# Decays of an S4 convolution precomputed through DRAM, its parameter tables in one pass, and side stages traced at other marks

## Chip, cores and metric

One core of one Trainium2 chip runs the whole program. The metric is the device time of one execution in microseconds (us); the kernel before was timed three times, and a fourth execution was taken with the profiler on. Differences are compared between executions of the same kind, and a profiled execution has its own time beside the span that its trace covers.

## What is computed

A layer norm of `x` (2048 rows of 576 channels) feeds two branches whose results are added to `x`:

```python
xn = layernorm(x)                                  # (2048, 576)
# branch A: S4 convolution along the sequence, per channel d, 128 states n
dt = exp(log_dt);  logdA = dt * (A_re + 1j*A_im);  dB = dt * (B_re + 1j*B_im)
K[d, l] = sum_n (C_re + 1j*C_im)[d,n] * exp(logdA[d,n] * l) * dB[d,n]   # real part, l = 0..2047
y = causal convolution of xn with K (by FFT, length 4096) + xn * Dskip
# branch B: feed-forward
out = silu(xn @ w1) @ w2                           # 576 -> 4608 -> 576
return x + y + out
```

All inputs and outputs are fp32.

## The kernel before, in words

**Main work.** `ffn` (line 223) computes branch B. Each fp32 operand is split into a high and a low part, and three products replace one. The hidden dimension is cut into 9 chunks of 512 (`c`), the 2048 rows into two halves of two blocks of 512. For every block, the four `up` steps (line 273) make hidden tiles: 14 matmuls of 512 columns, then on ScalarE (ACT) a Silu (`gf`, line 289) and a rounding copy (`gh`, line 290), then on VectorE (DVE) the low part (`gl`, line 291). The four `down` steps (line 293) multiply by `w2`: 24 matmuls of 288 columns, and DVE adds the results to `acc` (line 310). The steps run u0, d0, d1, d2, d3, u1, u2, u3, where the ups belong to the next block, so between the Silu of u0 and that of u1 lie four down steps. There are 288 steps in all. The weights of the next chunk are split on ACT and DVE (lines 250, 252, 268, 270).

**Side work.** `side` (line 699) is a generator with everything else. `weave` (line 31) resumes it between two main steps when the main work has reached the fraction of the 288 steps that the generator yielded last. Its stages are:

1. `phase0` (line 194): load rows, normalise, transpose on TensorE (PE). Rows 0 to 7 before the main loop, rows 8 to 15 inside it.
2. `natural` (line 370): the parameter tables. In two halves of 96 partitions x 384 values it forms `dt*A`, and the modulus and phase of `C*dB`, and turns four tables by PE transposes (`ptk`, line 452) into the layout [128 states, 576 channels]: `lrT` (real part of the log decay), `fT`, `rhoT`, `phiT`. ACT uses Abs, Sqrt (line 426) and Arctan (line 434) for it; Sqrt and Arctan each bring an `ACT_TABLE_LOAD`, and so does the Silu that follows.
3. `kgen` (line 455): the response K in 36 chunks of 16 channels, in pairs. `powers` (line 478) makes, once a pair, the decays `exp(lr*256), exp(lr*64), exp(lr*8), exp(lr)` as (1+tanh)/(1-tanh): a product with the lags on DVE (line 484), Tanh on ACT (485), and 1-t, a reciprocal and a fused product on DVE (486, 487, 490), then their powers up to 7 (492 to 494). `head` makes phases, ACT their sines and cosines (517 to 521), DVE the products `S` and `C` (522 to 538), and PE the sums `kp` and `z` (558, 573). The results go to DRAM as `d1k`. `spread` (line 133) does the first FFT stage of `xn` beside it.
4. `spectral` (line 592): 32 iterations of loads, splits, PE products `pk`, `pu`, `pb` (line 671), results to DRAM `d2` (line 632).
5. `tail` (line 637): reads `d2` back as `ys` (line 678) with a lead of `AHEAD` = 6 row tiles, and `add_conv` (line 681) does the last FFT stage on PE (`py`, line 691) and adds it. Rows 0 to 7 are added here, rows 8 to 15 in the last `down` steps of `ffn`.

The marks in `side` say where stages 3 to 5 are traced: `marks = (0.14, 0.65, 0.875, 0.905, 0.945)` are the fractions of the main steps at which kgen begins, kgen ends and spectral begins, spectral ends, the tail begins and the tail ends.

**Order.** Engines run their instructions in a fixed order. A planner fixes it ahead of the run by simulating a timeline with its own cost estimates; an instruction traced earlier, or inside `tc.high_priority()`, goes first among those that are ready. `behind(ins)` (line 130) keeps an instruction behind `ins` on the same engine. All loads of the side stages go through SyncE's queue (SP), in which the weight loads stand too; GpSimd's queue (POOL) carries the `d1u` and `d2` writes.

Of the kernel before, what the change touches and what calls it, by code (L numbers as in the profile page):

```python
# [10 lines left out]
F32 = mybir.dt.float32  # L11
# [6 lines left out]
P = 128  # L18
# [23 lines left out]
def kernel(  # L42
# [40 lines left out]
    dr0 = dram.tile([8 * P, D], F32, name="dr0")  # L83

# [6 lines left out]
    nc.vector.memset(halfpi, math.pi / 2)  # L91
    mhalf = cst.tile([P, 2], F32, name="mhalf")
# [130 lines left out]
    def ffn():  # L223
# [38 lines left out]
        def split_w2(half, c, t):  # L262
            first = half == 0 and c == 0
            r2 = R2.pop((half, c, t))
            h2 = wp.tile([P, D], F32R, tag="w2h", name="w2h", bufs=FT + 1)
            l2 = wp.tile([P, D], F32R, tag="w2l", name="w2l", bufs=FT + 1)
            with behind(pins["xt_s"] if first else pins["gh"]):
                nc.scalar.copy(h2, r2)  # L268
            with behind(pins["w1l"] if first else None):
                nc.vector.tensor_sub(l2, r2, h2)  # L270
            W2[half, c, t] = h2, l2
# [98 lines left out]
    def natural(nat):  # L370
        lrT, fT, rhoT, phiT = (kf[n] for n in ("lr", "f", "rho", "phi"))
        for half in range(2):
            NT = 3
            NP = 96
            ts = slice(half * NT, (half + 1) * NT)

            def load(ap, name):
                t = nat.tile([NP, NT, NS], F32, tag=name, name=name)
                nc.sync.dma_start(t, ap.rearrange("(p t) n -> p t n", t=6)[:, ts, :])
                return t  # L380

            are, aim = load(a_re, "are"), load(a_im, "aim")
            br, bi = load(b_re, "br"), load(b_im, "bi")
            cr, ci = load(c_re, "cr"), load(c_im, "ci")
            dt = nat.tile([NP, NT], F32, tag="dt", name="dt")
            nc.sync.dma_start(dt, log_dt.rearrange("(p t) -> p t", t=6)[:, ts])

            e1 = nat.tile([NP, NT], F32, tag="e1", name="e1")
            e2 = nat.tile([NP, NT], F32, tag="e2", name="e2")
            ec = float(np.float32(math.e))  # L390
            nc.vector.memset(e1, ec)
            nc.vector.tensor_scalar(e2, dt, 1.0 - math.log(ec), 1.0, op0=ALU.mult, op1=ALU.add)
            nc.gpsimd.tensor_tensor(e1, e1, dt, op=ALU.pow)
            nc.vector.tensor_mul(dt, e1, e2)
            dtb = dt.unsqueeze(2).broadcast_to([NP, NT, NS])
            v = nc.vector

            def tl(name):
                return nat.tile([NP, NT, NS], F32, tag=name, name=name)

            dh = nat.tile([NP, NT], F32, tag="dh", name="dh")
            nc.vector.tensor_scalar(dh, dt, 0.5, None, op0=ALU.mult)
            dhb = dh.unsqueeze(2).broadcast_to([NP, NT, NS])
            v.tensor_mul(are, are, dtb)
            nc.scalar.mul(aim, aim, 1.0 / (2 * math.pi))
            v.tensor_mul(aim, aim, dtb)
            pr, pi, t0, t1 = tl("pr"), tl("pi"), tl("t0"), tl("t1")
            v.tensor_mul(pr, cr, br)
            v.tensor_mul(t0, ci, bi)
            v.tensor_sub(pr, pr, t0)  # L410
            v.tensor_mul(pi, cr, bi)
            v.tensor_mul(t0, ci, br)
            v.tensor_add(pi, pi, t0)

            nc.scalar.activation(cr, pr, AF.Abs)
            nc.scalar.activation(ci, pi, AF.Abs)
            v.tensor_tensor(br, cr, ci, op=ALU.max)
            v.tensor_tensor(bi, cr, ci, op=ALU.min)
            v.tensor_scalar(t0, br, 1e-37, None, op0=ALU.max)
            v.reciprocal(t0, t0)  # L420
            v.tensor_mul(t0, t0, bi)
            v.tensor_scalar(t0, t0, 1.0, None, op0=ALU.min)

            v.tensor_mul(t1, t0, t0)
            v.tensor_scalar(t1, t1, 1.0, None, op0=ALU.add)
            nc.scalar.activation(bi, t1, AF.Sqrt)
            rc = tl("rc")
            v.reciprocal(rc, bi)
            v.tensor_mul(rc, rc, t1)
            v.tensor_add(bi, bi, rc)  # L430
            v.tensor_mul(br, br, bi)
            v.tensor_mul(br, br, dhb)

            nc.scalar.activation(t0, t0, AF.Arctan)
            nc.scalar.mul(t0, t0, 1.0 / (2 * math.pi))
            v.tensor_tensor(rc, ci, cr, op=ALU.is_gt)
            v.tensor_scalar(t1, t0, -2.0, 0.25, op0=ALU.mult, op1=ALU.add)
            v.tensor_mul(t1, t1, rc)
            v.tensor_add(t0, t0, t1)
            v.tensor_scalar(rc, pr, 0.0, None, op0=ALU.is_lt)  # L440
            v.tensor_scalar(t1, t0, -2.0, 0.5, op0=ALU.mult, op1=ALU.add)
            v.tensor_mul(t1, t1, rc)
            v.tensor_add(t0, t0, t1)
            v.tensor_scalar(rc, pi, 0.0, None, op0=ALU.is_lt)
            v.tensor_scalar(rc, rc, 2.0, -1.0, op0=ALU.mult, op1=ALU.add)
            v.tensor_mul(t0, t0, rc)
            yield half
            for src, dst in ((are, lrT), (aim, fT), (br, rhoT), (t0, phiT)):
                dv = dst.rearrange("n (p t) -> n t p", t=6)
                pt = pss.tile([P, 512], F32, tag="pss", name="ptk")  # L450
                for i in range(3):
                    nc.tensor.transpose(pt[:, i * NP:(i + 1) * NP], src[:, i, :], ident[:NP, :NP])
                nc.scalar.copy(dv[:, ts, :], pt[:, :3 * NP].rearrange("n (i p) -> n i p", i=3))

    def kgen():
        lrT, fT, rhoT, phiT = (kf[n] for n in ("lr", "f", "rho", "phi"))
        with tc.tile_pool(name="kg", bufs=1) as kg:
# [19 lines left out]

            def powers(i):

                ms = kg.tile([P, 2, W, 4], F32, tag="ms", name="ms")  # L480
                md = kg.tile([P, 2, W, 4], F32, tag="md", name="md")
                al = kg.tile([P, 2, W, 4], F32, tag="al", name="al", bufs=2)
                for q in range(2):
                    nc.vector.tensor_mul(split(ms[:, q]), row(vt[:, 65:69], 4), col(lrT, i + q, 4))
                nc.scalar.activation(ms, ms, AF.Tanh, scale=0.5)
                nc.vector.tensor_scalar(md, ms, -1.0, 1.0, op0=ALU.mult, op1=ALU.add)
                nc.vector.reciprocal(md, md)
                pv = pw.rearrange("n r d k e -> n (r d k) e")
                R = 2 * W * 4
                nc.vector.scalar_tensor_tensor(pv[:, :, 1], ms.rearrange("n r d k -> n (r d k)"), 1.0,  # L490
                                               md.rearrange("n r d k -> n (r d k)"), op0=ALU.add, op1=ALU.mult)
# [206 lines left out]

    def side():
        nonlocal s4, kl, yp, pa  # L700
        marks = (0.14, 0.65, 0.875, 0.905, 0.945)
# [8 lines left out]
        with tc.tile_pool(name="kf", bufs=1) as kfp:  # L710
            for n in ("lr", "f", "rho", "phi"):
# [125 lines left out]
```

## Time and profile before

| | us |
|---|---|
| median of three runs | 1140.75 |
| the three runs | 1139.23, 1140.75, 1143.12 |
| profiled execution, its own time | 1136.48 |
| span of its trace | 1134.7 |
| VectorE busy in the span | 939.5 |
| ScalarE busy in the span | 708.0 |
| mean granted TensorE clock | 0.995 |

The profiled execution ran 4.3 us below the median of the runs. The busy time of PE counts a matmul from its start to its modelled end, and matmuls overlap, so a full PE row doesn't by itself mean that PE runs at its rate; gaps, waits and the granted clock have to be read beside it.

### The profile page before, as it was taken

How to read it: one execution, taken by the hardware profiler on the slowest of the kernel's cores; microseconds unless marked ns; L12 is line 12 of the kernel's file. 1: busy time of each engine (PE TensorE's matmuls, PEld its weight loads, DVE VectorE, ACT ScalarE, POOL GpSimd, SP SyncE). 2: the span in 40 equal slices, each digit the busy share in tenths (PEclk: the TensorE clock that was granted, in tenths of full speed). 3: DMA queues.
4: the chain of work that ended last, by engine and by line, in shares of the span. 5: the costliest groups of instructions: out<-in, count | busy, mean ns of one | idle time of the engine just before them, and what ended most of it. 6: DMA issues, size and time to landing. Idle time of an engine off the chain costs nothing.

```text
span 1134.7 us, 22990 instructions
## 1 busy us (share of the span) xinstructions
PE 1112.0 (98%) x9184; PEld 1003.2 (88%) x9184; DVE 939.5 (83%) x1649; ACT 708.0 (62%) x1236; POOL 71.7 (6%) x131
## 2 busy tenths in 40 slices
PE   6999999999999999999999999999999999999998
PEld 5988899998989898999898989899999999999957
DVE  7788899999999999999899995587778787777434
ACT  5454646656657666666666674578877777787400
POOL 2100000000000000000000000000000000000021
PEclk9999999999999999999999999999999999999989
DMA  8365312324215143456733242754545454442596
GB/s 261 115 187 187 114 32 79 80 89 99 92 53 127 64 93 96 93 179 173 217 80 109 67 103 57 214 154 141 162 136 152 132 180 144 147 139 74 163 269 196
DMA packets 156203, 148.89 MB, mean 131 GB/s; under 512 B 82512, under 2 KB 123616, under 8 KB 155584
## 3 DMA queue, kind: packets, MB, share of 16 engines
q1 hardware_dynamic: 145872, 110.30, 34.9%
q0 software_dynamic: 9840, 36.24, 9.6%
q8 instruction: 72, 1.18, 0.4%
q10 hardware_dynamic: 384, 0.89, 0.3%
q14 instruction: 35, 0.29, 0.1%
HBM read 102.56 MB, written 44.90 MB: 130 GB/s over the span
## 4 chain that ended last, share of the span: by engine, by line
PE 80%; DVE 7%; DMA 6%; issue 4%; ACT 2%; SPq 1%; ACTq 0%; DVEq 0%; POOLq 0%
PE po L306 34%; PE ph L281 28%; PE kp L558 3%; PE ph L283 2%; PE pk L671 2%; PE ph L282 2%; PE pu L671 2%; PE pb L671 2%; PE z L573 2%; DMA w1r<-in_B_w_dram 1%; PE py L691 1%; DMA ys<-d 1%; PE pu L149 1%; DMA w2r<-in_B_w_dram 1%; DMA acc<-in_A_u_dram 1%
## 5 line engine op out<-in xcount | busy, mean ns | idle before, releaser
L306 PE MATMUL po<-w2h,gh 128*128 128x288 f32 x1152 | 337.4, 297 | 2.5 <-ACT gh L290 2.0
L306 PE MATMUL po<-w2l,gh 128*128 128x288 f32 x1152 | 337.2, 296 | 0.0
L306 PE MATMUL po<-w2h,gl 128*128 128x288 f32 x1152 | 333.5, 296 | 0.6 <-DVE gl L291 0.6
L306 PEld LDWEIGHTS po<-w2h,gh 128*128 128x128 f32 x1152 | 215.2, 188 | 12.2 <-issue 2.8
L306 PEld LDWEIGHTS po<-w2l,gh 128*128 128x128 f32 x1152 | 215.8, 188 | 5.2 <-issue 0.9
L306 PEld LDWEIGHTS po<-w2h,gl 128*128 128x128 f32 x1152 | 214.4, 188 | 1.9 <-DVE gl L291 0.9
L281 PE MATMUL ph<-xh,w1h 128*128 128x512 f32 (+1 forms) x592 | 163.3, 392 | 0.3 <-ACT xh L119 0.3
L281 PE MATMUL ph<-xl,w1h 128*128 128x512 f32 (+1 forms) x592 | 161.6, 388 | 0.0
L281 PE MATMUL ph<-xh,w1l 128*128 128x512 f32 (+1 forms) x592 | 159.9, 386 | 0.0
L310 DVE TENSOR_TENSOR acc<-po,acc 128x288 f32<-128x288 f32 x288 | 126.5, 452 | 28.8 <-PE po L306 27.1
L289 ACT ACTIVATE gf<-ph 128x512 f32<-128x512 f32 (+1 forms) x148 | 86.4, 584 | 97.0 <-PE ph L283 83.9
L281 PEld LDWEIGHTS ph<-xl,w1h 128*128 128x128 f32 x592 | 109.6, 190 | 22.0 <-issue 0.9
L291 DVE TENSOR_TENSOR gl<-gf,gh 128x512 fp32r<-128x512 f32 (+1 forms) x148 | 99.1, 673 | 34.5 <-ACT gh L290 33.9
L281 PEld LDWEIGHTS ph<-xh,w1l 128*128 128x128 f32 x592 | 107.9, 188 | 20.9 <-issue 0.9
L281 PEld LDWEIGHTS ph<-xh,w1h 128*128 128x128 f32 x592 | 106.2, 192 | 16.8 <-issue 0.7
L290 ACT CAST gh<-gf 128x512 fp32r<-128x512 f32 (+1 forms) x148 | 90.0, 609 | 25.7 <-PE po L306 23.1
L517 ACT ACTIVATE c<-th,magic 128x1040 f32<-128x1040 f32 x36 | 42.1, 1169 | 48.2 <-DVE C L538 26.8
L252 DVE TENSOR_TENSOR w1l<-w1r,w1h 128x640 fp32r<-128x640 f32 x72 | 57.0, 818 | 5.7 <-ACT w1h L250 5.5
L519 ACT ACTIVATE c<-th 128x1040 f32<-128x1040 f32 x36 | 38.7, 1076 | 33.3 <-DVE th L518 33.1
L268 ACT CAST w2h<-w2r 128x576 fp32r<-128x576 f32 x72 | 46.9, 674 | 18.0 <-DMA w2r<-in_B_w_dram 14.6
L283 PE MATMUL ph<-x,w1l 128*128 128x512 f32 (+1 forms) x148 | 57.0, 385 | 0.0
L282 PE MATMUL ph<-x,w1h 128*128 128x512 f32 (+1 forms) x148 | 56.9, 385 | 0.0
(176 smaller groups left out, 1869.2 us busy)
## 6 DMA issues: line engine op xcount, KB each, us to landing
w2r<-in_B_w_dram SPq DMA_DIRECT2D x72, 288.0 KB, 3.0
w1r<-in_B_w_dram SPq DMA_DIRECT2D x35, 512.0 KB, 3.9
d1u<-u POOLq DMA_DIRECT2D x32, 288.0 KB, 2.7
d1k<-stage SPq DMA_DIRECT2D x18, 512.0 KB, 8.1
ur<-d1u SPq DMA_DIRECT2D x32, 288.0 KB, 3.6
kr<-d1k SPq DMA_DIRECT2D x32, 288.0 KB, 2.7
d<-yo POOLq DMA_DIRECT2D x32, 288.0 KB, 3.2
ys<-d SPq DMA_DIRECT2D x32, 288.0 KB, 11.0
```

What stands on the lines that cost most here:

```text
L252: pins["w1l"] = nc.vector.tensor_sub(l1, src, h1).ins
L268: nc.scalar.copy(h2, r2)
L281: nc.tensor.matmul(ph, w[:, kt, :], v[:, kt, a:e], start=n + kt == 0, stop=False)
L282: nc.tensor.matmul(ph, h1[:, 4, :], x4[:, a:e], start=False, stop=False)
L283: pins["pe"] = nc.tensor.matmul(ph, l1[:, 4, :], x4[:, a:e], start=False, stop=True).ins
L289: nc.scalar.activation(gf, ph, AF.Silu)
L290: pins["gh"] = nc.scalar.copy(gh, gf).ins
L291: pins["gl"] = nc.vector.tensor_sub(gl, gf, gh).ins
L306: pins["pe"] = nc.tensor.matmul(po[:, :HD], G[blk, t][g][:, js], W2[half, c, t][w][:, hs], start=n == 0, stop=n == 3 * FT - 1).ins
L310: nc.vector.tensor_add(acc[j][:, hs], po[:, :HD], acc[j][:, hs])
L517: nc.scalar.activation(c65, th, AF.Identity, bias=magic)
L671: nc.tensor.matmul(dst, st, mv[:, hs], start=n == 0, stop=n == 3 * len(terms) - 1)
```

## The change

- A DRAM tensor `dexp` and a constant `neg1` are added. The decays of all 576 channels and four lags are made once: Tanh on ACT from the turned table `lrT`, then 1/(t-1)^2 as the square of an absolute reciprocal root, one correction and the quotient on DVE in four slices; the result `ex` is written to `dexp`.
- `powers` no longer makes the decays. It loads a pair's 128 values per state (`eb`, a pair ahead, through SP) and ACT copies them into the power table `pw`.
- `natural` works on 96 x 768 values in one pass, cut by three yields. The second and the third ACT block that need other tables are placed by `gate_of` just behind the Silu and copy of a u0 step. The square root, its reciprocal and their sum (lines 426 to 430) become an absolute reciprocal root and five DVE instructions.
- The tables' parts and `phase0` of rows 8 to 15 are traced at new fractions, and the five marks become `(0.13, 0.58, 0.81, 0.915, 0.955)`.
- `norm` writes rows 8 to 15 over the loaded rows.

```diff
+    dexp = dram.tile([P, 4 * D], F32, name="dexp")
...
+    neg1 = cst.tile([P, 1], F32, name="neg1")
+    nc.vector.memset(neg1, -1.0)
...
-        xn = p0.tile([P, 2, D], F32, tag="xn", name="xn")
+        xn = p0.tile([P, 2, D], F32, tag="xn", name="xn") if js[0] < 8 else pairs[js[0]]
...
     def natural(nat):
-        for half in range(2):
-            NT = 3
...
+        NT, NP = 6, 96
...
+        def turned(src, dst):
+            dv = dst.rearrange("n (p t) -> n t p", t=NT)
+            for h in range(2):
+                ts = slice(3 * h, 3 * h + 3)
                 pt = pss.tile([P, 512], F32, tag="pss", name="ptk")
                 for i in range(3):
...
+        dt = nat.tile([NP, NT], F32, tag="dt", name="dt")
+        nc.sync.dma_start(dt, log_dt.rearrange("(p t) -> p t", t=NT))
+        are, aim = load(a_re, "are"), load(a_im, "aim")
...
+        lrT = nat.tile([P, D], F32, tag="lrT", name="lrT")
+        turned(are, lrT)
+        turned(aim, fT)
+        ex = nat.tile([P, 4 * D], F32, tag="ex", name="ex")
+        r = nat.tile([P, 4 * D], F32, tag="r", name="r")
+        for k, lag in enumerate((256.0, 64.0, 8.0, 1.0)):
+            nc.scalar.activation(ex.rearrange("n (d k) -> n k d", k=4)[:, k, :], lrT, AF.Tanh, scale=0.5 * lag)
+        yield
+        with behind(pins["gh"]):
+            nc.scalar.activation(r, ex, AF.Abs_reciprocal_sqrt, bias=neg1)
+        nc.scalar.activation(r, r, AF.Square)
+        for i in range(0, 4 * D, D):
+            c = slice(i, i + D)
+            e = nat.tile([P, D], F32, tag="lrT", name="e")
+            v.scalar_tensor_tensor(e, ex[:, c], 1.0, r[:, c], op0=ALU.subtract, op1=ALU.mult)
+            v.scalar_tensor_tensor(r[:, c], e, 2.0, r[:, c], op0=ALU.add, op1=ALU.mult)
+            v.scalar_tensor_tensor(ex[:, c], ex[:, c], 1.0, r[:, c], op0=ALU.add, op1=ALU.mult)
+        nc.sync.dma_start(dexp, ex)
...
+        for i in range(0, NT, 2):
+            v.reciprocal(t0[:, i:i + 2], t0[:, i:i + 2])
...
+        yield
+        with behind(pins["gh"]):
+            last = nc.scalar.activation(t0, t0, AF.Arctan).ins
+        with behind(last):
+            last = nc.scalar.activation(bi, t1, AF.Abs_reciprocal_sqrt).ins
+        rc = tl("are")
+        v.tensor_mul(rc, t1, bi)
+        sq = tl("aim")
+        v.tensor_mul(sq, rc, rc)
+        v.tensor_sub(sq, t1, sq)
+        v.tensor_mul(sq, sq, bi)
+        v.scalar_tensor_tensor(bi, rc, 2.0, sq, op0=ALU.mult, op1=ALU.add)
...
+        with behind(last):
+            nc.scalar.mul(t0, t0, 1.0 / (2 * math.pi))
+        yield
...
+        turned(br, rhoT)
+        turned(t0, phiT)
...
+            def load_bases(i):
+                if i < NCK:
+                    bases.append(kg.tile([P, 2, W, 4], F32, tag="eb", name="eb", bufs=2))
+                    nc.sync.dma_start(bases[-1].rearrange("n g c k -> n g (c k)"),
+                                      dexp.rearrange("n (g r) -> n g r", g=2)[:, :, i * CH * 4:(i + 2) * CH * 4])
+            load_bases(0)
             def powers(i):
-                ms = kg.tile([P, 2, W, 4], F32, tag="ms", name="ms")
-                md = kg.tile([P, 2, W, 4], F32, tag="md", name="md")
                 al = kg.tile([P, 2, W, 4], F32, tag="al", name="al", bufs=2)
-                for q in range(2):
-                    nc.vector.tensor_mul(split(ms[:, q]), row(vt[:, 65:69], 4), col(lrT, i + q, 4))
-                nc.scalar.activation(ms, ms, AF.Tanh, scale=0.5)
-                nc.vector.tensor_scalar(md, ms, -1.0, 1.0, op0=ALU.mult, op1=ALU.add)
-                nc.vector.reciprocal(md, md)
+                load_bases(i + 2)
+                nc.scalar.copy(pw[:, :, :, :, 1].rearrange("n q (g c) k -> n q g (c k)", g=2),
+                               bases.pop(0).rearrange("n g (q c) k -> n q g (c k)", q=2))
                 pv = pw.rearrange("n r d k e -> n (r d k) e")
-                nc.vector.scalar_tensor_tensor(pv[:, :, 1], ms.rearrange("n r d k -> n (r d k)"), 1.0,
-                                               md.rearrange("n r d k -> n (r d k)"), op0=ALU.add, op1=ALU.mult)
                 nc.vector.tensor_mul(pv[:, :, 2], pv[:, :, 1], pv[:, :, 1])
...
+    def gate_of(i):
+        return (FT + i * 2 * FT + 1) / (2 * NCH * 2 * 2 * FT)
...
-        marks = (0.14, 0.65, 0.875, 0.905, 0.945)
+        marks = (0.13, 0.58, 0.81, 0.915, 0.955)
...
-                for i in range(4):
-                    if i % 2 == 0:
-                        next(nt, None)
-                    yield 0.03 + 0.014 * i
-                    with behind(pins["gl"]):
-                        phase0(pb, (8 + 2 * i, 9 + 2 * i))
-                    yield 0.037 + 0.014 * i
-                next(nt, None)
+                for at, tables in ((0.0, 1), (0.02, 0), (0.035, 0), (gate_of(1), 1), (0.06, 0), (gate_of(2), 1), (0.08, 0), (0.085, 1)):
+                    yield at
+                    if tables:
+                        next(nt, None)
+                    else:
+                        j = next(tiles)
+                        with behind(pins["gl"]):
+                            phase0(pb, (j, j + 1))
```

More of the change, by code (lines that the diff above doesn't have):

```diff
@@ L267, in split_w2 @@
             with behind(pins["xt_s"] if first else pins["gh"]):
-                nc.scalar.copy(h2, r2)
+                pins["w2h"] = nc.scalar.copy(h2, r2).ins
             with behind(pins["w1l"] if first else None):
@@ L370, in natural @@
     def natural(nat):
-        lrT, fT, rhoT, phiT = (kf[n] for n in ("lr", "f", "rho", "phi"))
-        for half in range(2):
-            NT = 3
[L374 to L449, printed above, removed]
@@ new lines, in natural, with tl, load @@
+        fT, rhoT, phiT = (kf[n] for n in ("f", "rho", "phi"))
+        NT, NP = 6, 96
+        v = nc.vector
+        def tl(name):
+            return nat.tile([NP, NT, NS], F32, tag=name, name=name)
+        def load(ap, name):
+            t = tl(name)
+            nc.sync.dma_start(t, ap.rearrange("(p t) n -> p t n", t=NT))
+            return t
+        def turned(src, dst):
+            dv = dst.rearrange("n (p t) -> n t p", t=NT)
+            for h in range(2):
+                ts = slice(3 * h, 3 * h + 3)
@@ new lines, in natural @@
+        are, aim = load(a_re, "are"), load(a_im, "aim")
+        br, bi = load(b_re, "br"), load(b_im, "bi")
+        cr, ci = load(c_re, "cr"), load(c_im, "ci")
+        e1 = nat.tile([NP, NT], F32, tag="e1", name="e1")
+        e2 = nat.tile([NP, NT], F32, tag="e2", name="e2")
+        ec = float(np.float32(math.e))
+        v.memset(e1, ec)
+        v.tensor_scalar(e2, dt, 1.0 - math.log(ec), 1.0, op0=ALU.mult, op1=ALU.add)
+        nc.gpsimd.tensor_tensor(e1, e1, dt, op=ALU.pow)
+        v.tensor_mul(dt, e1, e2)
@@ L455, in kgen @@
+        v.tensor_mul(t1, t1, rc)
+        v.tensor_add(t0, t0, t1)
+        v.tensor_scalar(rc, pr, 0.0, None, op0=ALU.is_lt)
+        v.tensor_scalar(t1, t0, -2.0, 0.5, op0=ALU.mult, op1=ALU.add)
+        v.tensor_mul(t1, t1, rc)
+        v.tensor_add(t0, t0, t1)
+        v.tensor_scalar(rc, pi, 0.0, None, op0=ALU.is_lt)
+        v.tensor_scalar(rc, rc, 2.0, -1.0, op0=ALU.mult, op1=ALU.add)
+        v.tensor_mul(t0, t0, rc)
+        turned(br, rhoT)
+        turned(t0, phiT)
     def kgen():
-        lrT, fT, rhoT, phiT = (kf[n] for n in ("lr", "f", "rho", "phi"))
+        fT, rhoT, phiT = (kf[n] for n in ("f", "rho", "phi"))
@@ L710, in side @@
         with tc.tile_pool(name="kf", bufs=1) as kfp:
-            for n in ("lr", "f", "rho", "phi"):
+            for n in ("f", "rho", "phi"):
                 kf[n] = kfp.tile([P, D], F32, name=n + "T")
```

31 lines of the change are left out of this document (30 added, 1 removed).

## Prediction, made before the changed kernel was run

> **What bounds the kernel now.** I read first the page's first part, then the windows view over the stages, then what PE waited for, then the chain of waits.
>
> ```profile
> span 1134.7 us, 22990 instructions
> PE 1112.0 (98%) x9184; PEld 1003.2 (88%) x9184; DVE 939.5 (83%) x1649; ACT 708.0 (62%) x1236; POOL 71.7 (6%) x131
> ...
> 407.35 2.72 PE ph L281 x12
> 542.49 4.78 PE po L306 x36
> 1069.69 11.58 DMA ys<-d
> ```
>
> The page puts PE at 98%. Busy time alone doesn't prove that PE runs at its rate, but two links of the chain do: 12 matmuls of 512 columns take 2.72 us (227 ns each) and 36 of 288 columns take 4.78 us (133 ns each). An up step is thus 14 x 0.227 = 3.2 us and a down step 24 x 0.133 = 3.2 us. PE work is what the change leaves alone: before and after, 24 transposes make the tables, and `kp`, `z`, the spectral products and `py` keep their number. So the change can only win what PE loses by waiting or by a lower clock, and lose by new waits. The windows say where that is (columns: us, busy us and instructions of PE, PEld, DVE, ACT, POOL, granted clock, DMA share, GB/s).
>
> ```profile
> 40.00:112.00 72.00, 71.63 (x435) 64.32 (x434) 61.12 (x141) 35.79 (x62) 6.02 (x7) 1.00 0.56 171
> ...
> 115.65:118.00 2.35, 0.36 (x4) 0.13 (x2) 2.11 (x2) 2.34 (x6) 0.00 (x0) 1.00 0.00 0
> 118.00:122.00 4.00, 4.00 (x13) 3.22 (x14) 3.94 (x9) 2.93 (x6) 0.00 (x0) 0.57 0.00 0
> ...
> 180.00:660.00 480.00, 478.65 (x4737) 432.43 (x4737) 456.48 (x722) 314.43 (x471) 19.54 (x36) 1.00 0.39 107
> ...
> 700.00:730.00 30.00, 28.35 (x176) 25.11 (x175) 12.92 (x23) 13.45 (x25) 2.00 (x3) 1.00 0.71 184
> 730.00:1060.00 330.00, 330.00 (x2094) 307.29 (x2093) 260.99 (x477) 252.05 (x526) 24.47 (x45) 1.00 0.45 139
> ...
> 1077.00:1080.00 3.00, 1.19 (x23) 0.80 (x21) 0.69 (x1) 0.00 (x0) 0.00 (x0) 1.00 1.08 233
> 1080.00:1088.00 8.00, 7.37 (x56) 4.74 (x44) 1.28 (x3) 0.00 (x0) 0.00 (x0) 0.57 1.08 233
> ```
>
> From 730 to 1060 us PE has no gap at all. Two places lose time. **Place A**, at 115.65: PE stands for 2.0 us, and in the next 4 us the clock is 0.57, that is (1 - 0.57) x 4 / 0.5 = 3.4 us at half speed, a loss of 1.7 us. **Place B**, at 1077: 1.8 us idle and then 0.6 us, and (1 - 0.57) x 8 / 0.5 = 6.9 us at half speed, a loss of 3.4 us. A is worth 3.7 us, B 5.8 us, together 9.5 us. Between 700 and 730 another 1.65 us are idle, where the first spectral product waits for the response to come back from DRAM; the change keeps that chain.
>
> ```profile
> PE py L691 <- DMA ys<-d: 2.4, 2, 1.8
> PE po L306 <- ACT gh L290: 2.0, 1, 2.0
> ```
>
> The waits view names the two: at A the down step waits for the rounded Silu output on ACT, at B `py` waits for the reload of `d2`.
>
> **The change, part by part.**
>
> *Place A: ACT's tables.* ACT's timeline before A:
>
> ```profile
> 109.13 1.28 ACT L434 ACT_TABLE_LOAD   x1
> 112.21 0.53 ACT L434 ACTIVATE t<-t 96x384 f32<-96x384 f32 x1 [1.79 <-DVE t L424]
> 112.75 1.28 ACT L426 ACT_TABLE_LOAD   x1
> 114.05 0.53 ACT L426 ACTIVATE bi<-t 96x384 f32<-96x384 f32 x1
> 114.59 1.28 ACT L289 ACT_TABLE_LOAD   x1
> 115.89 0.60 ACT L289 ACTIVATE gf<-ph 128x512 f32<-128x512 f32 x1
> ...
> 117.26 0.62 ACT L290 CAST gh<-gf 128x512 fp32r<-128x512 f32 x1
> ```
>
> From 109.13 to 115.89 ACT is taken by three loads, two functions and a wait for DVE, and the Silu stands behind them. The same block of the first half of the tables, at 61 us, cost PE next to nothing (71.63 busy of 72.00 us from 40 to 112). The change makes two other blocks of it, each behind the Silu of a u0 step, with four down steps and one up step until the next Silu's input is complete: 5 x 3.2 = 16 us of cover. Their length comes from ACT's rows:
>
> ```profile
> L519 ACT ACTIVATE c<-th 128x1040 f32<-128x1040 f32 x36 | 38.7, 1076 | 33.3 <-DVE th L518 33.1
> ...
> L426 ACT ACTIVATE bi<-t 96x384 f32<-96x384 f32 x2 | 1.1, 528 | 0.0
> ```
>
> 656 more columns cost 548 ns, so 2304 columns cost about 1.08 + 1264 x 0.00084 = 2.1 us and 768 about 0.85 us. If each change of function loads a table, the first block is 1.28 + 2.1 + 2.1 + 1.28 = 6.8 us, the second 3 x 1.28 + 3 x 0.85 = 6.4 us. Both fit into 16 us, so I cost them at nothing. If the cover is gone, because DVE brings the Arctan's argument late and the block slides among the ups u1 to u3 (one Silu every 3.2 us), the price is that of A, 2.0 + 1.7 = 3.7 us. That can happen: between the two gates lie 8 steps, 26 us, and DVE's work for it is
>
> ```profile
> L412 DVE TENSOR_TENSOR t<-ci,br 96x384 f32<-96x384 f32 x2 | 1.1, 555 | 0.0
> ...
> L420 DVE RECIPROCAL t<-t 96x384 f32<-96x384 f32 x2 | 5.1, 2546 | 0.0
> L270 DVE TENSOR_TENSOR w2l<-w2r,w2h 128x576 fp32r<-128x576 f32 x72 | 53.2, 750 | 2.4 <-ACT w2h L268 2.2
> L310 DVE TENSOR_TENSOR acc<-po,acc 128x288 f32<-128x288 f32 x288 | 126.5, 452 | 28.8 <-PE po L306 27.1
> L291 DVE TENSOR_TENSOR gl<-gf,gh 128x512 fp32r<-128x512 f32 (+1 forms) x148 | 99.1, 673 | 34.5 <-ACT gh L290 33.9
> L252 DVE TENSOR_TENSOR w1l<-w1r,w1h 128x640 fp32r<-128x640 f32 x72 | 57.0, 818 | 5.7 <-ACT w1h L250 5.5
> ```
>
> 12 fused products of 576 columns at 0.75 (9.0 us), about ten of 768 columns (384 take 0.55, 576 take 0.75, so about 0.95; 9.5), the reciprocal (5.1), three cheap ones (1.5): 25 us, and the main work's 126.5 + 99.1 + 57.0 + 53.2 = 335.8 us over 288 steps, 1.17 a step, 9 more. That is 34 us in 26, so the block lands some 8 us late: still in the down steps, which last 13 us, but not by much.
>
> The two new transposes of the real part and the phase now follow their loads directly. Two waits bound that: nothing, if the planner's estimate of the load is right, and the 3 us that DVE waited for a table load there before (a row below). I take 1 us.
>
> *The response's generation.* Each pair of chunks loses these DVE rows:
>
> ```profile
> L487 DVE RECIPROCAL md<-md 128x128 f32<-128x128 f32 x18 | 17.0, 946 | 0.0
> ...
> L490 DVE SCALAR_TENSOR_TENSOR pw<-ms,md 128x128 f32<-128x128 f32 x18 | 7.3, 405 | 0.0
> ...
> L484 DVE TENSOR_TENSOR ms<-vt,lrT 128x64 f32<-128x64 f32 x36 | 6.4, 220 | 0.0
> ...
> L486 DVE TENSOR_SCALAR md<-ms 128x128 f32<-128x128 f32 x18 | 3.9, 219 | 0.1
> ...
> DVE pr L408 <- DMA cr<-in_A_C_re_dram: 3.1, 1, 3.1
> ...
> L558 PE MATMUL kp<-C x1152: 219/219/243, 174.2 to 699.2; 128*32 128x64 f32 x192
> ```
>
> Together 34.6 us, 1.92 a pair. By itself this is worth nothing on PE. It pays for the shorter stage: `kp` runs from 174.2 to 699.2 in 18 pairs, 30.8 us each, or 0.51 x 288 / 18 = 8.2 steps. The new marks give 0.45 x 288 / 18 = 7.2 steps, 27.7 us. DVE was busy 456.48 of 480 us there, 29.3 of 30.8 us a pair. After: 29.3 - 1.92 - 0.96 x 1.17 = 26.3 us of 27.7, 95% as before. So the stage should fit the new marks and end 0.07 x 288 x 3.2 = 64 us sooner. ACT loses a Tanh and gets a copy of the same 128 columns. The 18 loads of 64 KB and the one write of 1.2 MB are small beside 107 GB/s x 480 us = 51 MB, and stand a pair ahead in SP's queue; what waits behind them there are weight loads a chunk ahead.
>
> The new wait is that DVE's first power (line 492) follows ACT's copy, which follows DVE's last reading of the old powers. Behind it on DVE stand `acc` and `gl`, for which PE's down steps wait. The nearest row is DVE's wait for ACT's sine:
>
> ```profile
> DVE S L537 <- ACT th L520: 7.7, 9, 1.5
> ```
>
> 7.7 us in 16 pairs is 0.5 a pair, 1.5 the longest. At 0.5 it fits the 1.4 us that a pair leaves free; I take that, and 0.5 us of PE waits over the stage. At 1.5 the pairs are full.
>
> *Place B: spectral work and tail.*
>
> ```profile
> L671 PE MATMUL pk<-kh,mm x128: 288/294/403, 726.3 to 1048.5; 128*128 128x288 f32 x128
> ...
> L632 POOL DMA_DIRECT2D d<-yo x32: 542/542/552, 747.3 to 1062.4; - x32
> L678 SPq DMA_DIRECT2D ys<-d x32: 573/574/1623, 1067.7 to 1109.0; - x32
> ```
>
> The spectral stage takes 1062.4 - 726.3 = 336 us, 10.5 us an iteration, while its marks ask for 0.225 x 288 x 3.2 = 207 us plus 576 matmuls x 0.133 = 77 us, 284 us. So it runs by its own chain and ends late, and the reload `ys` starts at 1067.7, when the tail should be under way: that is wait B. With its start 64 us earlier and the same 336 us, it ends near 998, and the first tail step is moved later, from 0.905 to 0.915: 24.5 steps and sixteen `py` groups before the end, near 1030. The first six row tiles need 12 of the 32 loads, 12 / 32 x 41 = 16 us, plus 12 to land: they are there near 1030 at the latest, and the rest come as buffers free. B goes, with its low clock: -5.8 us. Next late is nothing that the profile shows; `py` keeps its own cost.
>
> *The rule on the clock.* The low clock follows a PE wait of 2.0 us at A and of 1.8 at B. The Trainium skill's page "TensorE: Matmul & The Clock Gate", section "HAM oscillation — how this bites in real kernels", asks for idle gaps of over about 3.4 us. This case's trace does not agree, 2.0 us being followed by a clock of 0.57.
>
> **The sum.** -3.7 - 5.8 + 1 + 0.5 = -8.0 us on 1136.5, so 1128.5 for a profiled execution; against the median 1140.75 that is **1132.7 us**.
>
> **The rivals.**
> 1. *A stays or is replaced*: the Arctan block slides among the ups. For it: 34 us of DVE work in 26 us. Against: the block at 61 us cost nothing. Gain 8.0 - 3.7 = 4.3: 1136.4.
> 2. *The tail isn't relieved*, because the generation is held by DVE and ends when it did. For it: DVE's 95%. Gain 2.2: 1138.5.
> 3. *Slower: DVE waits for ACT's copy in every pair.* The copy can stand behind a sine of 1.08 us and a Silu, and the wait is on DVE in front of `acc`. It decides from 1.4 us a pair on. At 2.5 us each pair is 1.1 us over, 18 x 1.1 = 20 us, all paid by PE if the planner has not seen it: 1132.7 + 20 = 1153.
> 4. *The low clock does not hang on the waits* and falls elsewhere as often: then 5.1 us of the gain are gone: 1137.8. The page named above would lead there, with its longer gap.
>
> **How the numbers follow.** Forecast 0.52; rival 1 0.17; rival 2 0.09; rival 3 0.14; rival 4 0.08. A measurement of this kernel can tell about 0.3% from no change, 3.4 us. Faster by over 0.3% (below 1137.3): the forecast but for a twentieth (0.49), rival 1 (0.17) and half of rival 4 (0.04): 0.70. Within 0.3%: that twentieth (0.03), rival 2 (0.09), the other half of 4 (0.04) and the mild end of 3 (0.01): 0.17. Slower: the rest of 3, 0.13. The range goes from 1127, all 9.5 us, the 1.65 us near 726 and half of the runs' spread of 4 us, to 1146, rival 3 at a third of its price: a tenth lies on either side.
>
> **What would show it.** Right: no PE wait above 1 us near 115 and 1077, the clock at 1.00 in both, the last `d2` write near 1000, `kp` pairs 27.7 us apart, DVE near 95% there. Wrong: PE waiting for `gh` behind a table load, for a transpose behind a load near 45 us, for `kp` behind `C` or `S`, or DVE waiting at line 492's successor for the copy; or the last `d2` write still after 1040.

## The result, and the profile after

The changed kernel takes 1143.01 us (median of 19 runs, 1141.1 to 1146.53), the kernel before 1139.3 us on the same chip (19 runs, 1134.94 to 1143.12). The ratio, taken run against run, is 1.0032, with a 95% interval of 1.0022 to 1.0041: slower by a third of a per cent, where 1132.7 us, faster, was forecast. The profiled execution took 1141.12 us, with a span of 1139.4 us.

The windows view, cut into stages, shows where PE loses time. Its columns are as in the prediction: us, busy us and instructions of PE, PEld, DVE, ACT, POOL, granted clock, DMA share, GB/s. First before, then after.

```profile
75.00:165.00 90.00, 87.64 (x535) 79.37 (x534) 81.03 (x170) 47.19 (x79) 3.79 (x5) 0.98 0.45 137
165.00:640.00 475.00, 473.65 (x4695) 427.48 (x4693) 451.18 (x713) 307.59 (x461) 19.00 (x35) 1.00 0.38 106
...
665.00:1020.00 355.00, 353.30 (x2460) 326.43 (x2459) 271.88 (x484) 258.68 (x522) 24.85 (x45) 1.00 0.47 143
1020.00:1110.00 90.00, 87.41 (x638) 71.58 (x636) 46.18 (x91) 34.71 (x70) 12.04 (x24) 0.96 0.62 175
```

```profile
75.00:165.00 90.00, 87.06 (x521) 77.78 (x521) 81.66 (x148) 48.00 (x76) 3.77 (x4) 1.00 0.50 150
165.00:640.00 475.00, 472.58 (x5023) 425.70 (x5024) 456.84 (x670) 323.73 (x487) 21.21 (x39) 1.00 0.42 111
...
665.00:1020.00 355.00, 355.00 (x2239) 329.75 (x2238) 271.94 (x495) 261.85 (x547) 25.01 (x46) 1.00 0.49 146
1020.00:1110.00 90.00, 83.50 (x613) 68.07 (x612) 33.35 (x67) 17.56 (x29) 9.36 (x20) 0.96 0.63 152
```

Count as lost what PE isn't busy, and beside it (1 - clock) times the length of the window. From 75 to 165 us that is 2.4 + 1.8 = 4.2 us before and 2.9 after; from 165 to 640, 1.4 and 2.4; from 665 to 1020, 1.7 and nothing; from 1020 to 1110, 2.6 + 3.6 = 6.2 before and 6.5 + 3.6 = 10.1 after. In that last stage part of the low clock falls into the waits themselves, where it costs nothing; without that part the losses are 5.8 (place B of the prediction) and 9.2 (worked out below). Three stages together have changed by -1.9 us, the last by +3.4. (The span grew by 4.7 us. Of the other 3.2 us only about 0.15 is idle time outside these windows. The rest is busy time: PE was busy for 1112.6 us, 0.6 more than before, though the low clock took some 2 us less. What makes it so is not settled.)

So the tail is the place. The windows of the kernel after, laid closely around its loss, and what PE waited for from 1000 to 1060 us (us in total, times, longest):

```profile
1030.00:1037.10 7.10, 0.60 (x4) 0.18 (x2) 0.06 (x1) 0.76 (x2) 0.00 (x0) 0.90 1.08 218
1037.10:1043.00 5.90, 5.90 (x19) 5.14 (x20) 2.68 (x5) 0.93 (x2) 0.00 (x0) 0.54 0.70 159
```

```profile
PE po L309 <- ACT w2h L271: 6.5, 1, 6.5
```

PE stands for 6.5 us and then goes at a clock of 0.54 for 5.9 us, which costs 0.46 x 5.9 = 2.7 us more: 9.2 us at one place, more than the forecast's whole gain of 8.0. The wait isn't for `ys`. A down step lacks the rounded half of a weight tile, `w2h`. The timelines of SP and of ACT say why (start, us, line, operation; in brackets the idle time before it and what ended that):

```profile
1007.99 2.11 SPq L681 DMA_DIRECT2D r<-dr  x4
1010.14 14.61 SPq L718 DMA_DIRECT2D ys<-d  x12
1025.57 0.35 SPq L262 DMA_DIRECT2D w2r<-in_B_w_dram  x1
1026.88 4.61 SPq L718 DMA_DIRECT2D ys<-d  x4
```

```profile
1025.26 0.60 ACT L292 ACTIVATE gf<-ph 128x512 f32<-128x512 f32 x1 [2.33 <-PE ph L286]
1036.34 0.67 ACT L271 CAST w2h<-w2r 128x576 fp32r<-128x576 f32 x1 [10.48 <-DMA w2r<-in_B_w_dram]
```

Between the loads of the tail, four of 576 KB for the residual (`r`) and the first `ys` of 288 KB each, there is one weight load. It is issued at 1025.57 and lands at 1036.34, 10.8 us later, against a median of 3.4 us over the whole kernel (the page's row of issues, below). ACT stands 10.48 us in front of it.

```profile
w2r<-in_B_w_dram SPq DMA_DIRECT2D x72, 288.0 KB, 3.4
...
ys<-d SPq DMA_DIRECT2D x32, 288.0 KB, 8.8
```

Why wasn't it there before? The weight loads of the last 130 us, by tile, before (from 1000 us on) and after (from 1005 on):

```profile
L259 SPq DMA_DIRECT2D w2r<-in_B_w_dram x5: 328/333/339, 1001.6 to 1061.8; - x5
```

```profile
L262 SPq DMA_DIRECT2D w2r<-in_B_w_dram x5: 333/334/352, 1025.6 to 1076.8; - x5
```

Before, the last weight load is issued at 1061.8 and the first `ys` at 1067.7: none met the reload. After, the reload begins at 1010.1, and all five come behind its first loads.

Most of what was forecast for the other stages came about. These are rows of the kernel after, by tile: the response's products, the spectral products, the last results to DRAM, the reload; then two windows, one inside the generation and one at the start of the spectral stage.

```profile
L598 PE MATMUL kp<-C x1152: 219/219/244, 168.1 to 640.4; 128*32 128x64 f32 x192
...
L711 PE MATMUL pk<-kh,mm x128: 288/294/302, 666.0 to 989.6; 128*128 128x288 f32 x128
...
L672 POOL DMA_DIRECT2D d<-yo x32: 542/542/552, 686.4 to 1003.1; - x32
...
L718 SPq DMA_DIRECT2D ys<-d x32: 573/606/1787, 1010.1 to 1083.3; - x32
```

```profile
180.00:660.00 480.00, 477.58 (x4966) 430.21 (x4966) 447.43 (x657) 319.44 (x481) 23.21 (x42) 1.00 0.43 113
...
640.00:700.00 60.00, 60.00 (x420) 54.70 (x409) 38.52 (x69) 35.88 (x73) 3.65 (x6) 1.00 0.61 173
```

### The profile page after: what moved, and what is told of

Same layout as the page of the kernel before. It is cut to its first block, busy times and chain, and to the rows that moved or that the text cites. A ratio compares the mean times of both kernels' runs of the same rounds, so it can differ in the third digit from the quotient of the medians.

```text
span 1139.4 us, 22908 instructions
## 1 busy us (share of the span) xinstructions
PE 1112.6 (98%) x9184; PEld 1003.4 (88%) x9184; DVE 917.1 (80%) x1540; ACT 708.7 (62%) x1235; POOL 74.8 (7%) x130
## 4 chain that ended last, share of the span: by engine, by line
PE 52%; issue 22%; DVE 13%; DMA 7%; ACT 3%; SPq 2%; POOL 1%; ACTq 0%; DVEq 0%; POOLq 0%
PE po L309 22%; PE ph L284 18%; PE pk L711 2%; PE pu L711 2%; PE pb L711 2%; DMA dxt<-xt 2%; PE ph L285 1%; PE ph L286 1%; DMA w2r<-in_B_w_dram 1%; DMA ys<-d 1%; PE py L731 1%; DVE gl L294 1%; DVE acc L313 1%; PE kp L598 1%; DVE w2l L273 1%
## 5 line engine op out<-in xcount | busy, mean ns | idle before, releaser
L273 DVE TENSOR_TENSOR w2l<-w2r,w2h 128x576 fp32r<-128x576 f32 x72 | 53.6, 750 | 15.6 <-ACT w2h L271 15.6
```

## Experiments

All kernels compute the full output. The ratios are against the kernel before on the same chip, run against run. Three theories for the 6.5 us stood at the outset. **Order** (the expectations say "queue"): the weight load stands behind `ys` on SP's queue, so `ys` on another queue frees it. **Bytes** ("bandwidth"): the transfers share the DMA engines, whichever queue issues them, and the load is late by what is in front of it or beside it. **Marks:** the new times of the stages do it, and with the old ones the saved DVE work would be a gain. A rival in the expectations, "generation", puts the loss into the denser stage of the response instead.

### e1: the reload on GpSimd's queue

```diff
-                nc.sync.dma_start(yss[j][64 * h:64 * h + 64],
+                nc.gpsimd.dma_start(yss[j][64 * h:64 * h + 64],
```

> The changed kernel, with the reload of d2 (ys) issued on GpSimd's queue instead of SyncE's. In the changed kernel the last weight load w2r of a chunk stands in SyncE's queue behind twelve ys loads, lands 10.7 us after its issue, and PE stands 6.9 us at 1030 and then runs at half clock. Theory queue (the load is late because it stands behind the ys loads in one queue): w2r lands in about 4 us again, the stall goes with its low clock, 9.3 us less than the changed kernel, about 1134, 0.5% faster than before. Rival bandwidth (the transfers of ys take the DMA engines, whatever the queue): w2r still takes about 10 us, the stall stays, the time stays near 1143. Rival generation (the loss is made in the denser stage of the response, not in the tail): the time falls, but by less than 2 us, since PE's later waits absorb it.

Measured: 1143.06 us, ratio 1.0049 (1.0035 to 1.0063). Rows of SP's and ACT's timelines:

```profile
1012.78 1.38 SPq L262 DMA_DIRECT2D w2r<-in_B_w_dram  x2
...
1032.63 0.67 ACT L271 CAST w2h<-w2r 128x576 fp32r<-128x576 f32 x1 [12.52 <-DMA w2r<-in_B_w_dram]
```

The load is issued 12.8 us sooner and lands only 3.7 us sooner, 19.9 us after its issue. PE waits 6.5 us as before (the trace names `gh` for it, which stands behind this rounding on ACT). The DMA view from 1005 to 1033 us shows both queues at work (queue: packets, MB, share of the 16 engines):

```profile
q1 hardware_dynamic: 2125, 3.81, 47.9%
q0 software_dynamic: 846, 3.17, 47.8%
```

These shares cover the whole stretch, in whose first 9 us SP's queue (q1) does most. From 1014 to 1032.6 us, with both at work, GpSimd's queue (q0) has 66.2% of the engines' time and SP's 38.0%: about as many packets (749 and 789), but GpSimd's are larger (2.80 MB against 1.69). Order alone fell; the reload takes from the weight load wherever it stands. The Trainium skill's page "DMA: Bandwidth & Descriptors", section "Issuing engines are not separate DMA queues", says that transfers from the different issuing engines run on the same 16 DMA engines and interleave; this trace agrees, with those 749 and 789 packets in the same 18.6 us.

### e2 and e6: fewer bytes in front

e2 traces the six first pairs of `ys` apart; e6 shortens the reload's lead.

```diff
         for j in range(AHEAD):
+            yield 2.75 + 0.04 * j
             conv_load(j)
```

> The changed kernel, with the first six row tiles of ys traced one at a time over steps 256 to 262 instead of all together; they stay on SyncE's queue, and five of them instead of twelve stand ahead of the weight load. Theory queue: the wait at 1030 shrinks with the number ahead, to 5/12 of its length or less, about 2 us, and the clock holds: 6 to 8 us faster than the changed kernel, 1135 to 1137. Rival bandwidth: the same bytes move in the same 25 us, so w2r is late by nearly as much: gain under 2 us. Rival generation: as in the run with ys on GpSimd, under 2 us.

```diff
-    AHEAD = 6
+    AHEAD = 3
```

> The changed kernel with AHEAD = 3: five buffers of ys instead of eight, six loads ahead of the weight load instead of twelve. Theory bytes: half the burst, so w2r lands about 7 us sooner than in the changed kernel and the stall of 6.9 us falls to about 3 or less: 4 to 7 us less than the changed kernel; a lead of three row tiles (about 15 us) is enough for py. Rival: the shorter lead makes py wait, by 1 to 2 us a tile, and the time is not lower than the changed kernel's.

Measured: e2 1138.39 us, ratio 1.0011 (1.0002 to 1.0020); e6 1140.67 us, 1.0007 (0.9993 to 1.0022). In e2 five `ys` went ahead of the weight load, in e6 six, and PE's wait fell from 6.5 to 3.4 and 4.6 us. Against the changed kernel's ratio that is a gain of 2.4 and 2.8 us, less than either expectation asked for (6 to 8 by the queue, 4 to 7 by the bytes) and, in e2, a little more than the bandwidth rival's 2. The marks of e2 let the weight load ahead of seven `ys`, but didn't spread the loads in time: five are issued within 3.6 us, the other eleven from 1017.57 on. A mark says where in the order of tracing a load stands, not when it is issued.

### e5: the weight load first

```diff
-            nc.sync.dma_start(r2, w2v[:, c * FT + t, :])
+            pins["w2r"] = nc.sync.dma_start(r2, w2v[:, c * FT + t, :]).ins
...
-        for j in range(AHEAD):
-            conv_load(j)
+        yield 2.83
+        with behind(pins["w2r"]):
+            for j in range(AHEAD):
+                conv_load(j)
```

> The changed kernel, with the first six row tiles of ys kept behind the last w2r load of the chunk in hand, on the same queue. With ys on GpSimd's queue the weight load still landed late and PE still stood 6.8 us, so the queue's order is not the cause; the theory now is the bytes: 4.7 MB of ys at some 230 GB/s keep all 16 DMA engines full for 20 us, and a weight load issued among or behind them shares them. Theory bytes, first come first served: w2r, issued ahead of ys, lands in 4 to 6 us, the stall at 1028 falls under 1 us and the clock holds: 8 to 9 us less than the changed kernel, 0.4 to 0.5% faster than before. Theory bytes, shared among all that is in flight: ys follows w2r by a microsecond, so w2r still takes about 10 us and the stall keeps 2 to 4 us, as in the spread run.

Measured: 1133.42 us, ratio **0.9943** (0.9923 to 0.9963): faster than both kernels. SP's and ACT's timelines, and below them two windows of this kernel:

```profile
1010.13 1.96 SPq L681 DMA_DIRECT2D r<-dr  x4
1013.52 0.35 SPq L262 DMA_DIRECT2D w2r<-in_B_w_dram  x1
1013.91 19.68 SPq L720 DMA_DIRECT2D ys<-d  x16
...
1022.73 0.68 ACT L271 CAST w2h<-w2r 128x576 fp32r<-128x576 f32 x1 [1.89 <-DMA w2r<-in_B_w_dram]
```

```profile
75.00:165.00 90.00, 87.33 (x511) 77.55 (x509) 79.63 (x145) 48.27 (x76) 3.77 (x4) 0.98 0.49 150
...
1020.00:1110.00 90.00, 90.00 (x656) 72.96 (x655) 34.93 (x70) 21.01 (x35) 9.71 (x20) 1.00 0.66 162
```

The edit puts the first `ys` behind one weight load and, by `yield 2.83`, traces them later: they start at 1013.91 in place of 1010.14, the weight load at 1013.52 in place of 1025.57. From 1020 to 1110 us PE is now busy for all of 90 us at full clock. The ratio falls from 1.0032 to 0.9943, by some 10 us with about 2.5 either way, in which the 9.2 us of the place fit. Nothing else of the change was undone; the generation is as it was (2.5 us lost from 165 to 640), so the rival that put the loss there falls. Of the two forecasts, the first has the stall and the time right and the landing wrong: the load takes 9.2 us, not 4 to 6, since four `r` are still in front of it. It is in time because it is issued 12 us sooner. The role of the bytes shows in a count over the kernels with the load on SP's queue: how many KB were issued from the first `r` load up to and with the weight load, and how long it took from that first issue to ACT's rounding.

| | KB up to the weight load | us | GB/s |
|---|---|---|---|
| e5: 4 `r`, no `ys` | 2592 | 1010.13 to 1022.73: 12.6 | 211 |
| e2: 4 `r`, 5 `ys` | 4032 | 1009.53 to 1029.62: 20.1 | 205 |
| e6: 4 `r`, 6 `ys` | 4320 | 1007.86 to 1029.29: 21.4 | 207 |
| after: 4 `r`, 12 `ys` | 6048 | 1007.99 to 1036.34: 28.4 | 218 |
| e1: 4 `r`, `ys` on the other queue | 2592 | 1009.32 to 1032.63: 23.3 | 114 |

On one queue the more bytes stand in front, the later the load lands, at 205 to 218 GB/s; with a second queue at work the same 2592 KB take about twice as long. The order isn't strict: in these stretches of the first four rows the DMA view has 3.55, 4.97, 5.36 and 6.89 MB, 0.7 to 0.9 MB more than stood in front, so some of the `ys` issued behind the weight load moved before it had landed. Order counts, then, but as bytes on the same engines: the theory of bytes holds.

### e3 and e4: the marks alone, and the change with the old marks

e3 is the kernel before with the new marks, e4 the kernel after with the old.

```diff
-        marks = (0.14, 0.65, 0.875, 0.905, 0.945)
+        marks = (0.13, 0.58, 0.81, 0.915, 0.955)
```

> The kernel before, with the five new marks alone. Theory queue: the collision comes with the marks, since the spectral stage ends some 60 us sooner: a stall of 6 to 9 us at about 1030, the ys wait at 1077 gone, the wait at 115 kept, the time 1 to 5 us over before. Rival generation (the decays' new path makes the loss): the marks alone win the 5.8 us of place B, about 1134. A further chance: without the shorter DVE work the generation doesn't fit its marks, ends later than 645, and no stall at 1030 appears.

> The changed kernel, with the five old marks. Theory queue: all 32 ys loads stand behind the last weight load again, no stall at 1030, the ys wait near 1077 of about 6 us with its low clock is back, the wait at 115 is gone: 1 to 4 us faster than before, about 1136 to 1138. Rival generation (the copy on ACT and the tables cost PE 3 to 4 us): as slow as the changed kernel, or 2 to 4 us over before.

Measured: e3 1152.42 us, ratio 1.0136 (1.0123 to 1.0150); e4 1142.51 us, 1.0054 (1.0042 to 1.0066). Two windows of e3, in the generation; then what PE waited for in e4:

```profile
180.00:350.00 170.00, 170.00 (x1759) 153.47 (x1756) 169.15 (x269) 113.05 (x169) 5.95 (x11) 1.00 0.35 90
...
570.00:640.00 70.00, 61.61 (x651) 54.47 (x653) 63.05 (x95) 42.14 (x62) 2.71 (x5) 0.95 0.41 113
```

```profile
PE py L731 <- DMA ys<-d: 10.3, 6, 3.3
```

In e3 DVE is busy for 169.15 of 170 us, and PE pays later, 8.4 us of 70: without the saved decays the shorter stage doesn't fit. Of its expectation only the further chance came: `kp` runs to 664.9, the reload starts at 1034.8, and no weight load makes PE wait in the tail. In e4 the reload is as late as before, no weight load makes PE wait in the tail either, and `py` waits 10.3 us for `ys` (2.4 before). Its time is the rival's, 0.54% over before, but not by the rival's cause; why `py` waits so much longer than before isn't shown. So neither half is a gain by itself, and the new marks, which move the reload into the weight loads, are also what takes away wait B. The theory of marks is half right: with the old ones the collision is gone (e4), but taking them back is no gain.

### e7 and e8: the loads of the decays on GpSimd's queue

SP stands 10.65 us near 139 us in front of a load of decays that waits for its buffer, with weight loads behind it. e7 moves these loads to GpSimd; e8 does that on top of e5.

```diff
-                    nc.sync.dma_start(bases[-1].rearrange("n g c k -> n g (c k)"),
+                    nc.gpsimd.dma_start(bases[-1].rearrange("n g c k -> n g (c k)"),
```

> The changed kernel, with the decays' reloads (eb) on GpSimd's queue. In the changed kernel SyncE stands for 10 us from 139 to 149 at an eb load that waits for its buffer, with three w2r loads behind it, and PE waits for w2h at 162 and 455. Theory eb (the added loads cost PE through SyncE's queue): those two waits go, 1 to 3 us less than the changed kernel. Rival: those waits come from DVE and ACT being behind, and nothing changes by more than 1 us; the stall at 1030 stays in both cases.

> Both edits, ys kept behind the weight load and eb on GpSimd's queue. If the two add: 9 to 12 us less than the changed kernel, 0.6 to 0.7% faster than before. If the eb reloads matter nothing: the same time as the hold alone.

Measured: e7 1145.38 us, ratio 1.0047 (1.0031 to 1.0063); e8 1137.9 us, 0.9987 (0.9974 to 1.0001). The stand on SP went, but the weight loads behind it were issued at 151.88 us, where they had been at 151.34: they waited for their own buffers. e7 is no faster than the changed kernel (their intervals overlap), as the rival had it; e8 is neither of the two times expected but 0.4% above e5, so there the loads cost more on GpSimd. What makes them dear there is not settled.

### e9 and e10: what is left of place A

In the kernel after PE waits 1.6 us near 98 us for a `w2h`, in e5 2.0 us. e9's expectation takes its load, behind four loads of input rows (`xj`), to land just as the Arctan block leaves ACT free. SP's and then ACT's rows of the kernel after say otherwise:

```profile
92.18 0.34 SPq L262 DMA_DIRECT2D w2r<-in_B_w_dram  x1
92.63 1.76 SPq L163 DMA_DIRECT2D xj<-in_A_u_dram  x4
94.49 0.37 SPq L262 DMA_DIRECT2D w2r<-in_B_w_dram  x1
```

```profile
94.65 1.28 ACT L460 ACT_TABLE_LOAD   x1
...
98.85 0.66 ACT L271 CAST w2h<-w2r 128x576 fp32r<-128x576 f32 x1
```

The four weight tiles of a chunk are loaded and rounded in order, through two buffers. Counted so, the rounding at 98.85 is that of the fourth tile, and its load is the one at 92.18, ahead of the rows; the load at 94.49 belongs to the next chunk. The fourth tile landed 3.1 us after its issue, at 95.3 (in e5 at 96.9), while the block of Arctan and reciprocal root held ACT from 94.65 on. So the load was not late, and the wait is the block's. From e5, e9 traces one pair of rows behind the block, e10 puts the block behind the next u0.

```diff
-(gate_of(1), 1), (0.06, 0), (gate_of(2), 1), (0.08, 0), (0.085, 1)
+(gate_of(1), 1), (gate_of(2), 1), (0.078, 0), (0.08, 0), (0.085, 1)
```

> The kernel with the weight load held ahead of the reloads, and besides the loads of one pair of input rows traced after the Arctan block (mark 0.078 in place of 0.06), so that the weight load of 95.4 us doesn't stand behind them. In the kernel it starts from, PE waits 2.0 us near 98 us for w2h (L271), whose load landed just as the Arctan block (95.56 to 99.85 us on ACT) left ACT free. Theory of the rows: the weight load was late because of the four row loads ahead of it; the wait near 98 us shrinks below 0.7 us, provided that the rounding of w2h goes ahead of the second function. Theory of the block: ACT couldn't have taken w2h before 99.8 us anyway; the wait stays at 1.6 to 2.0 us. Time by the first: ratio to the kernel before 0.992 to 0.994; by the second 0.994 to 0.996.

```diff
-(gate_of(1), 1), (0.06, 0), (gate_of(2), 1), (0.08, 0), (0.085, 1)
+(gate_of(1), 1), (0.06, 0), (0.08, 0), (gate_of(3), 1), (0.105, 1)
```

> The same base, with the block of Arctan and reciprocal root traced behind the next u0 step (step 29 in place of 21, some 26 us later), the row loads left where they were. Theory of the block: the wait of 2.0 us near 98 us goes, and shows again near 124 us if a weight is due there as well. Theory of the rows: the wait near 98 us stays at 1 us or more, ACT being free but the load late. If both end together by chance, either experiment leaves some 1.5 us. Time: ratio 0.991 to 0.996 by either, which can't tell them apart; the waits do.

Measured: e9 1130.97 us, ratio 0.9953 (0.9938 to 0.9969); e10 1140.53 us, 1.0039 (1.0021 to 1.0057). The window from 75 to 165 us, in e9 and then in e10; behind them ACT's timeline of e10, and what PE waited for in e10:

```profile
75.00:165.00 90.00, 89.86 (x550) 81.39 (x548) 83.08 (x150) 47.10 (x75) 3.30 (x4) 1.00 0.46 146
```

```profile
75.00:165.00 90.00, 88.91 (x552) 80.92 (x551) 72.55 (x136) 42.56 (x71) 2.98 (x4) 1.00 0.48 147
```

```profile
95.03 0.67 ACT L271 CAST w2h<-w2r 128x576 fp32r<-128x576 f32 x1 [0.94 <-DMA w2r<-in_B_w_dram]
...
1061.77 1.35 ACT L253 CAST w1h<-w1r 128x640 fp32r<-128x640 f32 x2 [7.86 <-DMA w1r<-in_B_w_dram]
```

```profile
PE py L733 <- DVE r L739: 5.1, 1, 5.1
```

With the block out of the way (e10) the tile is rounded as it lands, 3.4 us after its issue. PE still waits 1.1 us for it, but comes to this step at 94.7 us, where in the kernel after it comes at 97.9, so the 1.1 is no share of the 2.0. In e9 the load is issued at 87.76, 5.1 us ahead of the block (2.5 in the kernel after), and the rounding at 91.03 goes ahead of the block: nothing is left of the loss, 89.86 of 90 us at full clock. The rows stand behind this load on the queue in both kernels; what else let it go sooner in e9, the runs don't say. The medians don't show e9's early gain: its interval lies on e5's.

e10 is slow for another reason, which is the collision once more. The order of the tail has shifted, three loads of `w1r` are issued between `ys` from 1046.9 us on and take 11.2 to 14.1 us to land (6.0 to 6.4 in e9). ACT waits 7.86 us for them, DVE's `w1l` waits for ACT, and behind it on DVE stands the sum that frees the buffer of `py`: PE waits 5.1 us. e5 ordered one weight load before the reload, not all of them.

## Why the prediction was wrong

**Place B, the step that failed.** The reload was where the step had it: the last `d2` at 1003.1 (forecast 998), the first `ys` at 1010.1, and no wait of `py` for `ys`. What failed is the sentence behind it, "Next late is nothing that the profile shows". The prediction followed the reload to the one that waits for it and not to the others on its queue and on the DMA engines. Two rows of before held the answer: the reload runs at a DMA share of 1.08, and it began after the last weight load. Begun 58 us sooner, it met the last five `w2r` loads, and the first of them made PE wait. This load has a lead of some 15 us: in e1, where it was issued as soon as its buffer was free, at 1012.78, PE stood from 1028.0. The reload had more, as the first `py` comes at 1050.8 (not near 1030, as the step had it). B's -5.8 was right by itself; the term put at nothing behind it is +9.2 us. e5 shows it: with that one load ordered, the loss from 1020 to 1110 is gone and the ratio 0.9943, where the forecast's is 1132.7 / 1140.75 = 0.9930. That these two are so near is in part luck, since e5 gains nothing at A (it loses 4.5 us from 75 to 165, before 4.2) and 1.7 us that weren't foreseen (below). The part on the generation did look at what stands behind added loads on SP; the part on the tail did not.

**Place A, mis-sized.** -3.7 was taken; the windows give 4.2 - 2.9 = 1.3. The old wait at 115 us went, but the cover of 16 us was reckoned up to the next Silu alone. The block itself came as forecast, right behind the `gh` of its u0 step (at 94.65, without a wait for DVE), with table loads of 1.28 us and functions of 0.85. But a rounding of `w2h`, due within the down steps, stood behind it on ACT, its load having landed 3.5 us before. e9 shows that the whole can be had: 0.1 us lost.

**The generation was right in what it did, less so in price.** `kp` runs from 168.1 to 640.4, (640.4 - 168.1) / 17 = 27.8 us a pair (27.7 forecast); it ends 59 us sooner (64). DVE was busy 456.84 of the 475 us from 165 to 640, 96% (95 forecast). The wait for ACT's copy in front of the powers, rival 3's mechanism, does not appear among DVE's waits. PE loses 2.4 us from 165 to 640, 1.0 more than before, where 0.5 was taken. The stage does need the saved decays, as e3 shows.

**Spectral stage:** 666.0 to 1003.1, 337 us (336 forecast). Not foreseen: the 1.65 us near its start, which the change was said to keep, are gone; PE is busy 60.00 of 60 us from 640 to 700.

**Transposes near 45 us:** no wait of PE belongs to them; the +1 was not spent.

**The terms as measured:** -1.3 (A), -5.8 (B), +9.2 (the weight load), +1.0 (generation), -1.7 (spectral stage) and 0 (transposes) make +1.4 us. The sign is explained by them, and of the span's 4.7 us the rest is the unsettled time of the result section.

**The rivals.** Rival 1 came in part of its price, at A, but not by its mechanism: the block didn't slide. Rival 2 did not: the generation was not held. Rival 3 did not come. Rival 4 is not borne out as a whole: once the main work ran, a clock of 0.50 to 0.66 followed every single PE wait of 3.4 us or more that is told of here (after, e1, e2, e6, e7, e10), and the tail of e5 and e9, without a wait, has none (1.00 from 1020 to 1110 us). Its page, "TensorE: Matmul & The Clock Gate" of the Trainium skill, section "HAM oscillation — how this bites in real kernels", asks for gaps over about 3.4 us. The 6.5 us agree with it (0.54 behind them), the 2.0 us at A before don't (0.57); and the wait near 98 us, of 1.6 us in the kernel after, was followed by a clock of 1.00, as was one of 2.5 us in e3 (1.00 from 115 to 125 us). A wait of about 2 us can cost a low clock or not, and these runs don't say on what that hangs.

The slower result was to come from DVE, by the one rival on that side. It came from a load off the path, through ACT.

## What to carry to other kernels

Where a stage moves in time, take every transfer that it issues and ask which loads with a short lead it will now meet, on its queue and on any other; a large reload at full DMA share makes each of them late by the bytes in front of it. Order the short-lead load ahead by an explicit dependence; another queue didn't protect it here (e1), and other trace marks did so in part (e2). A cover is reckoned up to the first instruction that stands behind the moved block on its engine, not up to the next one of the same kind.

## What the runs showed of the hardware

Two things were not expected. A load of 288 KB with a median of 3.4 us took 10.8 us behind twelve `ys` on its own queue and 19.9 us with the `ys` on another, where the two queues moved about as many packets each, GpSimd's the larger ones. And the rate of a burst that fills all DMA engines depends on what it moves: in the kernel after, from 1030 to 1037 us, `ys` (rows of 1152 bytes) runs at 218 GB/s with a share of 1.08; while the `r` loads move (rows of 2304 bytes, two to a partition), the DMA view shows 334 to 415 GB/s. The runs show the two rates side by side and not what makes them differ.
